# Seven products of zeros before the first scores, another order of two evictions, and twelve instead of fourteen weights prepared beside attention

## The chip, the cores and the metric

The kernel runs on one core of a Trainium2 chip. The metric is the device time of one execution in microseconds (us). PE is TensorE (matrix products; PEld is its weight load), DVE is VectorE, ACT is ScalarE, POOL is GpSimd, and SP is the engine that here issues the transfers. Each engine works through its own instructions in order and waits for others by semaphores.

## The reference, cut to what matters

Attention runs over 8 batches and 8 heads with 512 local and 32 global tokens and a head dimension of 64. A local token sees the 32 global keys and the local keys within 32 places; a global token sees all. Its result, 4608 tokens of 512 numbers, goes through two dense layers with a softplus between them.

```python
k_all = concat([k_g, k_l]); v_all = concat([v_g, v_l])
out_g = sm(scale * q_g @ k_all.T) @ v_all
s_ll = where(abs(pos[:, None] - pos[None, :]) <= 32, scale * q_l @ k_l.T, -1e9)
out_l = sm(concat([scale * q_l @ k_g.T, s_ll])) @ v_all
x = concat([out_g, out_l]).transpose(0, 2, 1, 3).reshape(4608, 512)
h = x @ w_in                                    # 512 x 2048
g = maximum(h, 0) + log1p(exp(-abs(h)))         # softplus
return g @ w_out                                # 2048 x 512
```

## The kernel before

**Stages.** Heads go in 32 pairs. The first six pairs are worked alone, before the dense layers begin; this part is called attention below. Everything behind it is the dense layers, in blocks of 512 tokens (b = 0 to 8, the last one half), with the attention of the other 26 pairs woven in between by a list of due times. In a block, 16 tiles h of 128 features are computed from x, put through the softplus, and their products with w_out are summed in four output tiles o. ORDER sets how h tiles, o products and the woven pieces follow each other.

**Products.** Results in 32 bits come from two halves: a number is split in a high part, rounded for TensorE, and a low part, the rest. Each product of x and a weight, or of g and a weight, is three: high by high, high by low, and low by high. A tile's name ends in h for its high and in l for its low part (xh, xl, gh, gl).

**The weights.** w_in and w_out come as 64-bit numbers in 32 tiles, wi0 to wi15 and wo0 to wo15. Each is prepared once: ACT takes absolute values of one word (L537, tile wbits), DVE puts the bits of a 32-bit number together in three instructions (L546, L548, L551, in the raw tile), ACT rounds them to the high part (a cast, L556), and POOL subtracts to get the low part in two instructions of 128x256 (L560). The raw words of weight k lie in the home of weight k+1 of the same kind, so weight k+1 cannot be cast before POOL has read weight k's raw words. W_PRE weights are prepared beside attention, one per step; the rest follow in block 0 of the dense layers, in the order of a list (order_w), each begun a fixed number of items ahead of its use (W_AHEAD).

**Attention's steps.** There are 15 steps, 12 local ones (pair m, half a) and three for global queries. Step k goes through stages: 0 scores on PE (two mask products, then eight products of raw queries and keys), followed by the maxima on DVE (L174, L175) and the exps with their sums on ACT (L177), 1 the reciprocals of the sums on DVE (L183, L184), 2 weighing of the exps e on POOL (L189), 3 the transpose of the weighed scores to PSUM (tile t), 4 its eviction by ACT in two parts (L223, L224: p..gh, p..gl), 5 products with the values, 6 the split of the result in xa/xh and xl (L242, L248, L249). The loop at the end of the kernel calls stages of neighbouring steps for each k; the order of these calls is the order of the work on PE and, for most of it, on ACT and DVE. The Tile scheduler places POOL's work and SP's transfers. `soft` holds the maxima and exps that belong to the scores issued in this turn of the loop, `take` is the copy of the first scores of pair 6 from PSUM (s_ps6_0, L346), and `held` is the weight whose bits are made in this step and whose cast ends it.

Of the kernel before, what the change touches and what calls it, by code (L numbers as in the profile page):

```python
# [8 lines left out]
F32 = mybir.dt.float32  # L9
F32R = mybir.dt.float32r  # L10
BF16 = mybir.dt.bfloat16
I32 = mybir.dt.int32
AF = mybir.ActivationFunctionType
ALU = mybir.AluOpType
# [25 lines left out]
SLOTS = {6: (72, 75, 78, 86, 90), 7: (81, 87, 87, 94.5, 97), 8: (93.6, 100.4, 100.4, 109, 113.5)}  # L40
ORDER = "H O H H O G O H O H H O H O G O H O H H O H O G O H O H H O H H O G O O".split()
GW = 75
W_AHEAD = 13
W_PRE = 14
LOADS = 16
START = 76
RATE = 3
# [15 lines left out]
def moe_over_global_local_attention(  # L63
# [22 lines left out]

    nc.scalar.preload_act_table_set("natural_log_exp_and_others")

    identf = pl.tile([P, P], F32, tag="e", name="identf", bufs=2)
    mask = const.tile([P, 1024], BF16, name="mask")
    ident = const.tile([P, P], BF16, name="ident")
# [34 lines left out]

    def mm(*a, **k):
        order["pe"] = after(nc.tensor.matmul(*a, **k), "pe").ins  # L130


    M = B * H // 2
# [417 lines left out]
        note("dve", nc.vector.scalar_tensor_tensor(r, lo32, 29, a, op0=ALU.logical_shift_right, op1=ALU.bitwise_or))  # L551
        return r.bitcast(F32)

    def halves_w(kind, k, r):
        (wi if kind == "wi" else wo)[k] = o = pl.tile([P, 2, 512], F32R, tag=f"{kind}{k}", name=f"{kind}{k}", bufs=1)
        i = note("act", nc.scalar.copy(o[:, 0], r))  # L556
        if not tight:
            tc.keep_in_program_order(i)
        for c in (slice(0, 256), slice(256, 512)):
            nc.gpsimd.tensor_tensor(o[:, 1, c], r[:, c], o[:, 0, c].bitcast(F32), op=ALU.subtract)  # L560

    def output_banks():
        if "o" not in banks:
# [169 lines left out]
    def stage(k, f):  # L733
        if 0 <= k < n:
            steps[k][0][f](*steps[k][1])
# [5 lines left out]
    for k in range(-2, n):  # L741
        stage(k - 3, 6)
        stage(k + 2, 0)
        soft = st.pop("soft", None)
        if soft and k:
            soft()
        stage(k + 1, 1)
        low_parts()
        stage(k + 1, 2)
        if k == 0:  # L750
            stage(k, 3)
            stage(k, 4)
            soft()
            key_masks()
        if k == n - 2:
            pcs.pop(0)[1]()
        for f, *args in fetch.get(k, ()):
            f(*args)
        if held:
            r = bits_w(*held)  # L760
        stage(k - 2, 5)
        if k == n - 1:
            stage(k - 2, 6)
            low_parts()
        if k:
            stage(k, 3)
            stage(k, 4)
        if k == n - 2:
            st.pop("take")()
        if k == n - 1:  # L770
            stage(k - 1, 5)
            stage(k - 1, 6)
            low_parts()
            pcs.pop(0)[1]()
        if held:
            halves_w(*held[:2], r)
            held = None
        if wk[1] < W_PRE:
            held = order_w[wk[1]]
            held += (abs_w(*held),)  # L780
            wk[1] += 1
# [78 lines left out]
```

## Time and profile before

| what | value |
|---|---|
| median of 3 runs | 957.56 us |
| the runs | 958.10, 957.56, 957.14 us |
| the profiled execution's own time | 957.48 us |
| its span | 955.7 us |
| granted clock, mean | 1.0 |
| PE busy | 938.4 us (98%) |
| DVE busy | 621.1 us (65%) |
| ACT busy | 506.7 us (53%) |
| POOL busy | 455.6 us (48%) |

The durations and waits come from the profiled execution. A row of the timeline has a start in us from the span's start, the busy time in us, the engine, the source line, the operation, what is written and read with its shape, a count of instructions put together (x8), and in brackets the idle time of the engine before it with what ended that. A row of the waits names who waited for whom, and gives the us in total, the number of waits and the longest. The dense layers' first product starts at 75.80 us.

### The profile page before, as it was taken

What the parts mean: (1) busy time and instruction counts of PE and PEld (TensorE: products, weight loads), DVE (VectorE), ACT (ScalarE), POOL (GpSimd) and SP (SyncE); (2) the same over time, 40 slices, a digit from 0 to 9 for tenths busy, and PEclk for the clock granted to TensorE, in tenths of its full rate; (3) what the DMA queues carried; (4) which work ended last, traced back from release to release, by engine and by line L of the source; (5) the groups of instructions that cost most, each with busy time, mean ns of one, the idle gap of its engine ahead of it and who ended that gap; (6) DMA issues with size and microseconds to landing.
All of it is one profiled execution on the core that took longest, in us unless ns stands there. A gap on an engine that the chain in (4) does not pass through costs nothing.

```text
span 955.7 us, 14401 instructions
## 1 busy us (share of the span) xinstructions
PE 938.4 (98%) x5239; PEld 757.8 (79%) x5239; DVE 621.1 (65%) x1271; ACT 506.7 (53%) x914; POOL 455.6 (48%) x634
## 2 busy tenths in 40 slices
PE   6999999999999999999999999999999999999998
PEld 4777777878888888888888888878888888888896
DVE  7985899687677667777668667767767765211211
ACT  6897776744445446444445446444445445544453
POOL 6984897654435344444435345444435334222221
PEclk9999999999999999999999999999999999999999
DMA  9745421111112110211112111211112100100000
GB/s 355 272 139 174 146 91 43 66 51 51 51 51 94 35 51 18 95 51 51 51 51 95 42 43 31 96 37 51 51 51 95 50 2 19 50 1 1 23 23 23
DMA packets 34327, 66.21 MB, mean 69 GB/s; under 512 B 7632, under 2 KB 11472, under 8 KB 34256
## 3 DMA queue, kind: packets, MB, share of 16 engines
q1 hardware_dynamic: 33440, 65.19, 20.8%
q8 instruction: 41, 0.67, 0.3%
q14 instruction: 30, 0.25, 0.1%
q10 hardware_dynamic: 816, 0.10, 0.1%
HBM read 55.84 MB, written 9.44 MB: 68 GB/s over the span
## 4 chain that ended last, share of the span: by engine, by line
PE 84%; POOL 5%; ACT 5%; DVE 4%; issue 2%; POOLq 0%; ACTq 0%; DVEq 0%
PE o L130 36%; PE h L130 35%; PE s_ps L130 5%; PE v_ps L130 5%; POOL e L189 2%; PE s L130 1%; ACT xh L509 1%; POOL gl L608 1%; POOL wi L560 1%; DVE e L603 1%; PE o0g L130 1%; PE t L130 1%; ACT e L599 1%; POOL s L416 1%; ACT gh L606 1%
## 5 line engine op out<-in xcount | busy, mean ns | idle before, releaser
L130 PE MATMUL h<-xh,wi 128*128 128x512 f32 (+1 forms) x1152 | 343.2, 381 | 0.5 <-DVE e L603 0.4
L130 PE MATMUL o<-wo,gh 128*128 128x512 f32 x1088 | 343.4, 397 | 0.0
L608 POOL TENSOR_TENSOR gl<-e,gh 128x512 fp32r<-128x512 f32 (+1 forms) x152 | 182.4, 1204 | 258.9 <-ACT gh L606 224.5
L130 PEld LDWEIGHTS h<-xh,wi 128*128 128x128 f32 x1152 | 211.4, 188 | 46.9 <-DVE e L603 1.6
L130 PEld LDWEIGHTS o<-wo,gh 128*128 128x128 f32 x1088 | 200.3, 188 | 46.3
L130 PE MATMUL h<-xl,wi 128*128 128x512 f32 (+1 forms) x576 | 219.9, 382 | 0.0
L130 PE MATMUL o<-wo,gl 128*128 128x512 f32 x544 | 213.7, 393 | 0.0
L603 DVE SCALAR_TENSOR_TENSOR e<-h,e 128x512 f32<-128x512 f32 x136 | 92.8, 682 | 172.8 <-ACT e L601 157.3
L599 ACT ACTIVATE e<-h 128x512 f32<-128x512 f32 x136 | 80.8, 594 | 213.4 <-PE h L130 213.3
L416 POOL TENSOR_TENSOR s<-s,mb 128x320 f32<-128x320 f32 (+6 forms) x136 | 138.5, 1051 | 70.9 <-DVE mb L412 70.9
L606 ACT CAST gh<-e 128x512 fp32r<-128x512 f32 x136 | 84.0, 617 | 121.9 <-DVE e L603 121.9
L130 PEld LDWEIGHTS h<-xl,wi 128*128 128x128 f32 x576 | 108.1, 188 | 21.8
L130 PEld LDWEIGHTS o<-wo,gl 128*128 128x128 f32 x544 | 102.2, 188 | 23.7 <-POOL gl L608 0.2
L601 ACT ACTIVATE e<-e,one 128x512 f32<-128x512 f32 x136 | 98.4, 724 | 4.0
L430 DVE TRANSPOSE_TENSOR_REDUCE zt<-s 128x32 f32<-128x1024 f32 x52 | 64.7, 1244 | 53.1 <-ACT s L424 53.1
L600 ACT ACTIVATE e<-e 128x512 f32<-128x512 f32 x136 | 85.9, 631 | 3.1
L424 ACT ACTIVATE s<-s 128x1024 f32<-128x1024 f32 x52 | 55.1, 1060 | 28.6 <-POOL mt L341 24.1
L365 DVE TRANSPOSE_TENSOR_REDUCE mt<-s 128x32 f32<-128x1024 f32 x52 | 64.6, 1243 | 7.7 <-ACT s L346 6.1
L390 POOL COPY mt<-mt 32x75 f32<-32x75 f32 x78 | 19.2, 246 | 96.1 <-DVE mt L365 94.0
L130 PEld LDWEIGHTS s_ps<-raw 64*128 64x128 f32 x728 | 54.9, 187 | 12.3 <-issue 8.8
L130 PE MATMUL s_ps<-raw 64*128 64x192 f32 (+3 forms) x728 | 60.6, 308 | 1.0 <-DVE e L603 0.5
L412 DVE STREAM_TRANSPOSE mb<-mt 128x512 f32<-128x512 f32 (+1 forms) x104 | 52.8, 564 | 1.2 <-ACT mt L403 0.4
(129 smaller groups left out, 863.9 us busy)
## 6 DMA issues: line engine op xcount, KB each, us to landing
raw<-in_qk SPq DMA_DIRECT2D x52, 272.0 KB, 2.8
v<-in_v SPq DMA_DIRECT2D x26, 384.0 KB, 3.1
out<-ot SPq DMA_DIRECT2D x34, 256.0 KB, 2.2
wiraw<-in_w_in SPq DMA_DIRECT2D x16, 512.0 KB, 7.2
woraw<-in_w_out SPq DMA_DIRECT2D x16, 512.0 KB, 6.6
raw<-in_qk SPq DMA_DIRECT2D x26, 224.0 KB, 3.2
v<-in_v SPq DMA_DIRECT2D x6, 512.0 KB, 7.3
raw<-in_qk SPq DMA_DIRECT2D x6, 416.0 KB, 6.2
```

What stands on the lines that cost most here:

```text
L130: order["pe"] = after(nc.tensor.matmul(*a, **k), "pe").ins
L365: order["scores"] = nc.vector.tensor_reduce(windows(st["mt", m], 4 + 16 * g, 36, 2, 16), s.rearrange("p h (b k) -> p h b k", k=32), axis=A ...
L412: nc.vector.transpose(mb[:, :, o:o + 32 * n].rearrange("p h (s k) -> p h s k", k=32), windows(e, k, 21, 2, n).unsqueeze(3).to_broadcast([P ...
L416: i = nc.gpsimd.tensor_tensor(s[:, h, o:o + w], s[:, h, o:o + w], mb[:, h, q:q + w], op=ALU.subtract)
L424: i = nc.scalar.activation(s, s, AF.Exp, scale=0.125)
L430: nc.vector.tensor_reduce(windows(st["zt", m], 4 + 16 * g, 36, 2, 16), s.rearrange("p h (b k) -> p h b k", k=32), axis=AX.X, op=ALU.add, a ...
L599: nc.scalar.activation(e, ph, AF.Abs)
L600: nc.scalar.activation(e, e, AF.Exp, scale=-1.0)
L601: nc.scalar.activation(e, e, AF.Ln, bias=one)
L603: order["e"] = nc.vector.scalar_tensor_tensor(e, ph, 0.0, e, op0=ALU.max, op1=ALU.add).ins
L606: nc.scalar.copy(gh, e)
L608: nc.gpsimd.tensor_tensor(gl[:, c], e[:, c], gh[:, c].bitcast(F32), op=ALU.subtract)
```

## The change

It has four parts.

1. A tile of zeros of 128x512 bf16 is written by DVE, and PE multiplies it seven times with itself ahead of all other products. Nothing reads the result.
2. At step k=1 the transpose and the eviction of that step are called before `soft` (the exps of step 3, e0_1_1) and before stages 1 and 2 of step 2; the second weight's cast, kept back at k=0, stands behind that eviction, and its low part on POOL behind the weighing of step 2, e0_1_0 (the order rows below have the names).
3. The copy `take` moves from step n-2 to step n-1, behind the last evictions there.
4. W_PRE goes from 14 to 12 and W_AHEAD from 13 to 11: wo4 and wo5 are no longer prepared beside attention but first in block 0.

```diff
-W_AHEAD = 13
-W_PRE = 14
+W_AHEAD = 11
+W_PRE = 12
...
+    zeros = pl.tile([P, 512], BF16, tag="mb", name="zeros", bufs=2)
+    nc.vector.memset(zeros, 0.0)
+    idle = ps_h.tile([P, 512], F32, tag="h", name="idle")
+    for _ in range(7):
+        mm(idle, lhsT=zeros[:, :P], rhs=zeros, start=True, stop=True, skip_group_check=True)
...
-    def halves_w(kind, k, r):
+    def halves_w(kind, k, r, later=None):
         (wi if kind == "wi" else wo)[k] = o = pl.tile([P, 2, 512], F32R, tag=f"{kind}{k}", name=f"{kind}{k}", bufs=1)
         i = note("act", nc.scalar.copy(o[:, 0], r))
         if not tight:
             tc.keep_in_program_order(i)
-        for c in (slice(0, 256), slice(256, 512)):
-            nc.gpsimd.tensor_tensor(o[:, 1, c], r[:, c], o[:, 0, c].bitcast(F32), op=ALU.subtract)
+        def low():
+            for c in (slice(0, 256), slice(256, 512)):
+                nc.gpsimd.tensor_tensor(o[:, 1, c], r[:, c], o[:, 0, c].bitcast(F32), op=ALU.subtract)
+
+        low() if later is None else later.append(low)
...
         soft = st.pop("soft", None)
+        behind = []
+        if k == 1:
+            stage(k, 3)
+            stage(k, 4)
+            halves_w(*kept, behind)
         if soft and k:
             soft()
         stage(k + 1, 1)
         low_parts()
         stage(k + 1, 2)
+        for low in behind:
+            low()
         if k == 0:
...
-        if k:
+        if k not in (0, 1):
             stage(k, 3)
             stage(k, 4)
-        if k == n - 2:
+        if k == n - 1:
             st.pop("take")()
-        if k == n - 1:
             stage(k - 1, 5)
             stage(k - 1, 6)
             low_parts()
             pcs.pop(0)[1]()
-        if held:
+        if held and k == 0:
+            kept = (*held[:2], r)
+        elif held:
             halves_w(*held[:2], r)
-            held = None
+        held = None
```

Line numbers of the changed kernel stand six to nine above those of before (L560 becomes L567, L608 becomes L617).

On POOL, from the weighing of the second step (e0_0_1) on, before:

```order
L189 TENSOR_SCALAR e0_0_1_173<-e0_0_1_173,sums0_1_174 128x224 x4
L560 TENSOR_TENSOR wi0_190<-wiraw0_109,wi0_190 128x256 x2
L560 TENSOR_TENSOR wi1_270<-wiraw1_117,wi1_270 128x256 x2
L189 TENSOR_SCALAR e0_1_0_203<-e0_1_0_203,sums1_0_223 128x224 x4
L560 TENSOR_TENSOR wi2_313<-wiraw2_119,wi2_313 128x256 x2
```

and of the change:

```order
L195 TENSOR_SCALAR e0_0_1_183<-e0_0_1_183,sums0_1_184 128x224 x4
L567 TENSOR_TENSOR wi0_200<-wiraw0_119,wi0_200 128x256 x2
L195 TENSOR_SCALAR e0_1_0_213<-e0_1_0_213,sums1_0_233 128x224 x4
L567 TENSOR_TENSOR wi1_303<-wiraw1_127,wi1_303 128x256 x2
L195 TENSOR_SCALAR e0_1_1_289<-e0_1_1_289,sums1_1_305 128x224 x4
L567 TENSOR_TENSOR wi2_323<-wiraw2_129,wi2_323 128x256 x2
```

The low part of wi1 has gone behind the weighing of e0_1_0, and that of wi2 behind the weighing of e0_1_1.

On ACT, at the same place (the exps of e0_1_0, weights wi1 to wi3, and the eviction of t0_0_1), before:

```order
L177 ACTIVATE e0_1_0_203,sums1_0_223<-s0_1_0_196,sums1_0_223 128x224 x4
L556 CAST wi1_270<-wiraw1_117 128x512
L537 ACTIVATE wbitswi2_274<-wiraw2_119 128x512
L177 ACTIVATE e0_1_1_283,sums1_1_284<-s0_1_1_276,sums1_1_284 128x224 x4
L223 COPY p0_0_1gh_309<-t0_0_1_300 128x512
L224 COPY p0_0_1gl_310<-t0_0_1_300 96x512
L556 CAST wi2_313<-wiraw2_119 128x512
L537 ACTIVATE wbitswi3_317<-wiraw3_127 128x512
```

and of the change:

```order
L183 ACTIVATE e0_1_0_213,sums1_0_233<-s0_1_0_206,sums1_0_233 128x224 x4
L543 ACTIVATE wbitswi2_280<-wiraw2_129 128x512
L229 COPY p0_0_1gh_299<-t0_0_1_290 128x512
L230 COPY p0_0_1gl_300<-t0_0_1_290 96x512
L562 CAST wi1_303<-wiraw1_127 128x512
L183 ACTIVATE e0_1_1_289,sums1_1_305<-s0_1_1_282,sums1_1_305 128x224 x4
L562 CAST wi2_323<-wiraw2_129 128x512
L543 ACTIVATE wbitswi3_327<-wiraw3_137 128x512
```

The eviction and the cast of wi1 now stand ahead of the exps of e0_1_1, and wi2's absolute values ahead of both.

On POOL in block 0, around the low parts of gl0_9 and gl0_10 (the softplus results of hidden tiles 9 and 10), before:

```order
L560 TENSOR_TENSOR wi14_1548<-wiraw14_1318,wi14_1548 128x256 x2
L560 TENSOR_TENSOR wo10_1624<-woraw10_1345,wo10_1624 128x256 x2
L608 TENSOR_TENSOR gl0_9_1630<-e0_9_1620,gh0_9_1629 128x256 x2
L390 COPY zt7_1561<-zt7_1561 32x75 x3
L560 TENSOR_TENSOR wo11_1675<-woraw11_1394,wo11_1675 128x256 x2
L608 TENSOR_TENSOR gl0_10_1681<-e0_10_1671,gh0_10_1680 128x256 x2
L560 TENSOR_TENSOR wi15_1685<-wiraw15_1436,wi15_1685 128x256 x2
```

and of the change:

```order
L567 TENSOR_TENSOR wi13_1612<-wiraw13_1333,wi13_1612 128x256 x2
L617 TENSOR_TENSOR gl0_9_1618<-e0_9_1608,gh0_9_1617 128x256 x2
L396 COPY zt7_1549<-zt7_1549 32x75 x3
L567 TENSOR_TENSOR wi14_1663<-wiraw14_1382,wi14_1663 128x256 x2
L617 TENSOR_TENSOR gl0_10_1669<-e0_10_1659,gh0_10_1668 128x256 x2
L567 TENSOR_TENSOR wo10_1675<-woraw10_1424,wo10_1675 128x256 x2
```

Each weight stands two places later among the weights than before; wo10 now follows gl0_10, where it preceded gl0_9.

## The prediction

> **What bounds the kernel now.** I read the page's busy shares first, then the waits of PE, then busy time by stretch.
>
> ```profile
> PE 938.4 (98%) x5239; PEld 757.8 (79%) x5239; DVE 621.1 (65%) x1271; ACT 506.7 (53%) x914; POOL 455.6 (48%) x634
> ```
>
> TensorE is busy for 938.4 of 955.7 us, so some 17 us can be saved at most, and each new PE wait costs its own length. The waits of 10 to 76 us (first row) and of 74 to 200 us (the other two, all that PE waits for there) say where these gaps are:
>
> ```profile
> PE t L130 <- POOL e L189: 4.2, 3, 2.3
> PE s_ps L130 <- DVE e L603: 0.5, 1, 0.5
> PE h L130 <- DVE e L603: 0.4, 1, 0.4
> ```
>
> Attention (to 75.8 us) is not PE's to set; from there on PE sets the time alone. In the stretches of block 0 (start:end, length, then busy us of PE, PEld, DVE, ACT, POOL):
>
> ```profile
> 75.00:85.00 10.00, 10.00 (x60) 8.48 (x59) 3.88 (x8) 6.68 (x15) 3.09 (x7) 1.00 0.81 270
> 85.00:165.00 80.00, 79.55 (x397) 62.69 (x396) 72.68 (x108) 57.75 (x101) 68.61 (x84) 1.00 0.30 96
> 165.00:180.00 15.00, 15.00 (x76) 12.13 (x75) 10.28 (x20) 9.87 (x21) 8.81 (x13) 1.00 0.12 34
> ```
>
> From 85 to 165 us DVE has 7.3 and POOL 11.4 us left of 80, while PE has no gap but the 0.4. This is where the change puts more work.
>
> **The zeros.** The first memsets stand at
>
> ```profile
> 0.83 0.15 DVE L96 MEMSET mask<- 128x112 uint32 x1 [0.83 <-PEq L851]
> 1.00 0.34 DVE L108 MEMSET mask<- 128x336 uint32 x1
> 3.92 0.91 PE L130 MATMUL s<-mask,ident 128*128 128x448 bf16 x2 [3.92 <-DVE mask L104]
> 4.76 1.86 PE L130 MATMUL s<-raw 64*128 64x224 f32 x8
> ```
>
> Clearing 128x512 bf16 (256 words a row) lies between 0.15 and 0.34 us: 0.27, so the zeros begin at about 1.25 us. Two cold mask products start 0.84 apart, 0.42 for 448 columns, so 0.48 for 512 and 3.36 for seven. They end at 4.6 and move the first scores from 3.92 by +0.7 us. Against this stands the clock:
>
> ```profile
> 7.41 1.87 PE L130 MATMUL s<-raw 64*128 64x224 f32 x8
> 9.95 0.90 PE L130 MATMUL s<-mask,ident 128*128 128x448 bf16 x2 [0.67 <-ACT e L177]
> 12.57 1.60 PE L130 MATMUL t<-identf,e 128*128 128x128 f32 x8
> 14.48 1.03 PE L130 MATMUL s<-raw 64*128 64x224 f32 x8
> ```
>
> Eight raw products take 1.87 us early and 1.03 from 14.48 on; the transposes of 12.57 hold the change, at about 13.5. The 5.4 unbroken us from 3.92 did not bring it, the 3.5 from 9.95 did. A fixed grid of equal stretches fits both: 10.0 to 13.5 full, 6.6 to 10.0 broken by the 0.67, 3.1 to 6.6 begun before 3.92. With zeros from 1.25 the stretch 3.1 to 6.6 is full, so I take full speed at 6.6; if the grid lies otherwise, between 1.25+3.5 = 4.8 and 1.25+7 = 8.3. [...]
>
> What the faster scores are worth is set by the chain behind them:
>
> ```profile
> 8.07 0.45 ACT L177 ACTIVATE e<-s,sums 128x224 f32<-128x224 f32 x1 [6.06 <-DVE sums L175]
> 9.77 0.66 ACT L537 ACTIVATE wbitswi<-wiraw 128x512 f32<-128x512 f32 x1
> 10.82 0.40 DVE L546 TENSOR_SCALAR wbitswi<-wbitswi 128x512 int32<-128x512 int32 x1
> ```
>
> The first scores, mask and raw, end 2.7 us after they start (6.6). From 4.6 with the second half at full speed they end at 6.9, 0.3 later; the exps then start at 8.37, the weight's absolute values at 10.07, and its first bits at 10.75, where before the second reduction held them to 10.82: **-0.1**. Bounds: -0.9 (full speed at 4.8), +0.7 (no change of clock). The selects of the later masks, which POOL now does behind the first mask's, and the weight loads that change places on SP go at 0: the zeros end after the first mask is there (3.92), and none of the waits of PE quoted above is for a load. If one were late, its wait would show on ACT's first pass over that weight and cost what the third weight's does below.
>
> **The second eviction.** At k=1 POOL now weighs e1_0 right behind the first weight's low part, and prepares the second low part after it.
>
> ```profile
> 18.02 0.18 DVE L184 RECIPROCAL sums<-sums 128x4 f32<-128x4 f32 x1
> 19.18 0.49 DVE L546 TENSOR_SCALAR wbitswi<-wbitswi 128x512 int32<-128x512 int32 x1 [0.98 <-ACT wbitswi L537]
> 18.65 1.61 POOL L560 TENSOR_TENSOR wi<-wiraw,wi 128x256 fp32r<-128x256 f32 x2 [0.76 <-ACT wi L556]
> 20.25 2.60 POOL L189 TENSOR_SCALAR e<-e,sums 128x224 f32<-128x224 f32 x4
> 21.78 0.68 ACT L556 CAST wi<-wiraw 128x512 fp32r<-128x512 f32 x1
> 23.08 0.76 DVE L546 TENSOR_SCALAR wbitswi<-wbitswi 128x512 int32<-128x512 int32 x1
> 21.90 1.43 PE L130 MATMUL t<-identf,e 128*128 128x128 f32 x8 [2.33 <-POOL e L189]
> ```
>
> The weighing needs the reciprocal of 18.02: 18.25 to 20.85, two us earlier, and the 2.33 of PE shrinks. Behind it the low part runs to about 22.4, and only then may ACT cast the third weight, whose home holds the second's raw values: cast to 23.1 (before 22.4), the fourth's absolute values to 23.75, and DVE's bits from 23.8 where they stood at 23.08: +0.7, with the exps behind them +0.8. ACT stands still for some 1.3 us before that cast. DVE's 0.98 goes, as the third weight's absolute values now stand ahead of the cast of the second, but DVE then meets the later stall. What it loses there lasts, because it has no slack in the stretches that follow (columns as above):
>
> ```profile
> 23.00:57.00 34.00, 30.79 (x271) 23.06 (x272) 31.48 (x60) 29.99 (x92) 29.49 (x42) 1.00 0.73 261
> 57.00:69.50 12.50, 12.50 (x112) 10.40 (x109) 11.93 (x25) 11.26 (x35) 12.03 (x18) 1.00 0.18 48
> ```
>
> DVE is busy for 31.5 of 34 us and then 11.9 of 12.5, more than PE in the first, while PE fills the second whole. So I carry the stall to the end of attention: **+0.8**. Bounds: -0.1, if DVE uses all of the saved 0.98 on work that it can draw forward and meets the later cast 0.9 late, and +1.1, if the weighing too is 0.3 later than I put it, as the low part ahead of it took 1.86 there and not the 1.6 of the others.
>
> **The last eviction and the copy.**
>
> ```profile
> 71.61 1.02 ACT L346 COPY s<-s_ps 128x1024 f32<-128x1024 f32 x1
> 72.52 0.66 ACT L242 COPY xa<-o 128x256 f32<-128x256 f32 x2
> 72.96 0.44 PE L130 MATMUL o<-p_1gh,v 128*64 128x128 f32 x4 [0.40 <-ACT xa L242]
> ```
>
> The copy of 1.02 us moves behind the xa copies, for which PE waited 0.40 at 72.96 and stood 0.17 before 71.82: **-0.55**. Bounds 0 (the gap turns to the next eviction) and -0.9 (all that the copy takes from start to start).
>
> **Two weights less beside attention.** Their bits took DVE 4.7 us in six rows, first and last:
>
> ```profile
> 62.83 0.45 DVE L546 TENSOR_SCALAR wbitswo<-wbitswo 128x512 int32<-128x512 int32 x1
> 68.48 0.82 DVE L551 SCALAR_TENSOR_TENSOR woraw<-woraw,wbitswo 128x512 int32<-128x512 int32 x1
> ```
>
> They lie where PE has no gap (12.50 of 12.50 above), so their going is worth **0**: POOL and ACT, which lose a low part of 1.5 and two passes of 0.7 us for each, are off that path as well. Without this cover, that is if DVE did set the time there, it would be up to 4.7 us gained; PE's full row excludes it. Up to the first MoE product the sum is +0.15. In block 0 the two come first and every later weight moves two places back. The places of preparation among the other work on ACT, DVE and POOL stay what they were, so I use a rule of places: a weight is ready when the weight in its place was before. Where this brings one past its use is at wo10, which falls from ahead of gl0_9 to behind gl0_10 on POOL:
>
> ```profile
> 138.96 2.08 POOL L560 TENSOR_TENSOR wi<-wiraw,wi 128x256 fp32r<-128x256 f32 x2
> 141.01 2.35 POOL L560 TENSOR_TENSOR wo<-woraw,wo 128x256 fp32r<-128x256 f32 x2
> 146.69 1.47 POOL L560 TENSOR_TENSOR wo<-woraw,wo 128x256 fp32r<-128x256 f32 x2
> 149.71 1.46 POOL L560 TENSOR_TENSOR wi<-wiraw,wi 128x256 fp32r<-128x256 f32 x2
> 149.77 0.61 PE L130 MATMUL o<-wo,gh 128*128 128x512 f32 x2
> 154.12 2.18 POOL L560 TENSOR_TENSOR wo<-woraw,wo 128x256 fp32r<-128x256 f32 x2 [0.35 <-ACT wo L556]
> 157.38 0.61 PE L130 MATMUL o<-wo,gh 128*128 128x512 f32 x2
> 140.48 1.12 DVE L548 SCALAR_TENSOR_TENSOR wbitswo<-woraw,wbitswo 128x512 int32<-128x512 int32 x1
> ```
>
> Before, wo10 (141.01) was ready at 143.4 for its products at 149.77, the second of which, at 150.0, reads the low part. Now wi14 has the place of 146.69 and wo10 that of 149.71, which ends at 151.17: PE waits 1.2 us. That is the least. The pairs took 2.08 and 2.35 beside DVE's two-input shifts (140.48, 1.12 us), and 1.47 and 1.46 elsewhere; with two more weights' shifts to do DVE is at them then. wi14 and wo10 at 2.08 and 2.35 add 1.50, so I take **+2.7**; at 2.35 both, 2.9. [...]
>
> The next, wo11, comes in the place of 154.12, ready at 156.3 for products at 157.38; those behind it are no closer. PE's stall then moves their use back by its own length, so none of them adds. The 0.41 that PE waits for a softplus near 161 is covered by the stall: **-0.4** (bound 0). DVE carries 4.7 us more through block 0, and the idle left from 165 to 180 is 4.7 of 15; what is not taken up there lands on the 0.50 that PE waits near 192, for the same engine: **+0.6** (0 to 1.2).
>
> **Sum:** -0.1 +0.8 -0.55 +2.7 -0.4 +0.6 = +3.05 on the profiled 957.48 (span 955.7 and 1.8 around it), which stands 0.08 under the median of 957.56: **960.5 us**.
>
> **Rivals.** *wo10 is not late.* From 75 to 85 us DVE has 6.1 us idle; if the two extra weights are done in it, nothing moves, the terms of block 0 are zero, and the time is 957.48+0.15 = 957.6. For it speaks that idle time and POOL's 6.9. Against it: DVE's order puts their bits behind the second softplus, which comes at 85. *The start wins (faster).* The place is DVE's row at 19.18: its 0.98 goes, and if the low part is done by 21.8, when ACT wants the cast, nothing of it comes back. With the clock's -0.9 and the copy's -0.55 attention ends 2.4 earlier, and with wo10 in time as above the time is 955.0. It decides whether POOL ends that low part before 21.8; 20.85+1.6 says not. *DVE becomes the bound (slower still).* With 72.7+4.7 = 77.4 of 80 us it has 2.6 left, and each wait of its own for ACT delays a softplus. At the upper bounds of wo10 (2.9), of the second eviction (1.1) and of block 1 (1.2), nothing gained at 161 or by the copy, the time is 957.48+5.1 = 962.6. *The zeros don't change the clock,* the case in which the change doesn't do what it says: +0.7 for -0.1 gives 961.3.
>
> **How the numbers follow.** Chances: forecast 0.55 (959.0 to 962.0 its own range), wo10 in time 0.20, the fast start 0.09, DVE the bound 0.12, no change of clock 0.04. A measurement of this kernel can tell about 0.2%, 1.9 us, from no change: under 955.6 is faster, over 959.5 slower. Faster holds the fast start, 0.09; the same holds wo10 in time and the forecast's lowest 0.06, 0.26; slower the rest, 0.65. The range of 956.6 to 962.4 leaves out most of the fast start and half of the slowest case.
>
> **What would show it.** Raw products of 1.03 us from 6.6 on; ACT idle before a cast at about 22; xa copies ahead of the s copy at 72; the first h product near 76.0 (75.8 before); and above all a PE wait of 1.2 to 2.9 us for POOL's wo row near 150. If PE shows no wait there, the forecast is wrong by its largest term; if the wait stands but the time is no longer, the start gave more than I grant.

## The result and the profile after

The changed kernel takes 964.61 us (median of 6 runs, 963.73 to 965.09), the kernel before 957.40 us on the same chip (6 runs). The ratio is 1.0073, with a 95% interval of 1.0063 to 1.0084: slower by 7.2 us. The forecast was 960.5 us, at most 962.4. The profiled execution of the change took 965.09 us, its span is 963.2.

The busy shares of the change, then all waits of PE from 74 to 205 us (PE's products stand at L130 before and at L128 in the change):

```profile
PE 940.1 (98%) x5242; PEld 758.0 (79%) x5246; DVE 624.4 (65%) x1272; ACT 506.3 (53%) x914; POOL 457.1 (47%) x634
```

```profile
PE o L128 <- POOL gl L617: 1.9, 1, 1.9
PE h L128 <- DVE e L612: 1.4, 2, 1.1
PE o L128 <- ACT gh L615: 1.1, 1, 1.1
PE s_ps L128 <- DVE e L612: 0.5, 1, 0.5
PE o L128 <- POOL wo L567: 0.2, 1, 0.2
```

PE is as busy as before but for 1.7 us, and it has four waits that it had not: for gl0_9 (1.9), for softplus results (1.1 and 0.3 beside the old 0.4 that is gone), for gh (1.1). The wait for wo10, the largest term of the forecast, is 0.2. A second loss shows in the granted clock (stretch, length, busy us of PE, PEld, DVE, ACT, POOL, clock):

```profile
85.00:145.00 60.00, 59.36 (x294) 47.02 (x296) 52.20 (x78) 42.78 (x75) 52.75 (x63) 1.00 0.32 102
145.00:165.00 20.00, 17.88 (x85) 13.66 (x84) 19.51 (x28) 13.10 (x26) 16.07 (x21) 0.91 0.19 57
165.00:180.00 15.00, 15.00 (x76) 12.13 (x75) 13.42 (x17) 11.15 (x22) 12.17 (x14) 1.00 0.23 76
180.00:205.00 25.00, 22.18 (x111) 17.06 (x110) 17.64 (x33) 13.64 (x28) 13.00 (x21) 1.00 0.22 74
```

The timeline of PE shows both losses, one behind the other:

```profile
147.62 0.50 PE L128 MATMUL o<-wo,gl 128*128 128x512 f32 x1 [1.90 <-POOL gl L617]
147.96 0.62 PE L128 MATMUL o<-wo,gh 128*128 128x512 f32 x2
...
149.81 1.05 PE L128 MATMUL o<-wo,gh 128*128 128x512 f32 x2
...
151.09 1.05 PE L128 MATMUL h<-xh,wi 128*128 128x512 f32 x2
...
152.30 0.62 PE L128 MATMUL h<-xh,wi 128*128 128x512 f32 x2
```

A pair of products takes 0.62 us, then 1.05, then 0.62 again: for some 3.4 us PE worked at half its clock (granted 0.50 from 148.79 to 152.21). From 147.96 to 152.30 it needed 4.34 us for what took 3.05 before (144.64 to 147.69), 1.29 lost.

Following the same product through both traces gives the whole sum of the change, as lateness against before: 0.61 at the first dense product (76.41 for 75.80), 0.62 more by 141 us (wait for a softplus), 2.09 at gl0_9, 1.29 by the clock, 0.51 at wo10, 0.66 back near 160 (where before PE waited 0.41), and 3.01 at two waits in the beginning of block 1 (184.56 and 191.88). That is 7.47, and from 205 us on the lateness stays at 7.5.

POOL's queue ahead of gl0_9, before and in the change:

```profile
135.77 3.19 POOL L416 TENSOR_TENSOR s<-s,mb 128x384 f32<-128x384 f32 x3
138.96 2.08 POOL L560 TENSOR_TENSOR wi<-wiraw,wi 128x256 fp32r<-128x256 f32 x2
141.01 2.35 POOL L560 TENSOR_TENSOR wo<-woraw,wo 128x256 fp32r<-128x256 f32 x2
143.33 1.63 POOL L608 TENSOR_TENSOR gl<-e,gh 128x256 fp32r<-128x256 f32 x2
```

```profile
138.82 1.94 POOL L567 TENSOR_TENSOR wi<-wiraw,wi 128x256 fp32r<-128x256 f32 x2
140.72 3.67 POOL L422 TENSOR_TENSOR s<-s,mb 128x384 f32<-128x384 f32 x3
144.39 2.04 POOL L567 TENSOR_TENSOR wi<-wiraw,wi 128x256 fp32r<-128x256 f32 x2
146.39 1.88 POOL L617 TENSOR_TENSOR gl<-e,gh 128x256 fp32r<-128x256 f32 x2
```

Before, the selects s of pair 7 ended at 138.9 and gl0_9 began at 143.33. Now wi12's low part stands ahead of these selects, wi13's behind them; the selects begin 5.0 us later than before, and gl0_9 comes 3.1 us later.

### The profile page after: what moved, and what is told of

Its sections match the earlier page's. It is cut to its first block, busy times and chain, and to the rows that moved or that the text cites. A ratio compares the mean times of both kernels' runs of the same rounds, so it can differ in the third digit from the quotient of the medians.

```text
span 963.2 us, 14406 instructions
## 1 busy us (share of the span) xinstructions
PE 940.1 (98%) x5242; PEld 758.0 (79%) x5246; DVE 624.4 (65%) x1272; ACT 506.3 (53%) x914; POOL 457.1 (47%) x634
## 4 chain that ended last, share of the span: by engine, by line
PE 82%; POOL 5%; ACT 5%; DVE 3%; issue 3%; DMA 1%; SPq 0%; POOLq 0%; ACTq 0%; DVEq 0%
PE o L128 35%; PE h L128 34%; PE s_ps L128 5%; PE v_ps L128 5%; POOL gl L617 1%; POOL s L422 1%; ACT xh L515 1%; DMA wiraw<-in_w_in 1%; PE o0g L128 1%; ACT e L608 1%; POOL wo L567 1%; PE t L128 1%; DVE e L612 1%; POOL e L195 1%; PE s L128 1%
## 5 line engine op out<-in xcount | busy, mean ns | idle before, releaser
L128 PE MATMUL o<-wo,gh 128*128 128x512 f32 x1088 | 344.6, 398 | 1.3 <-ACT gh L615 1.1
L128 PE MATMUL h<-xh,wi 128*128 128x512 f32 (+1 forms) x1152 | 343.5, 381 | 1.4 <-DVE e L612 1.4
L617 POOL TENSOR_TENSOR gl<-e,gh 128x512 fp32r<-128x512 f32 (+1 forms) x152 | 185.6, 1225 | 265.3 <-ACT gh L615 227.7
L128 PEld LDWEIGHTS h<-xh,wi 128*128 128x128 f32 x1152 | 211.8, 188 | 48.0 <-DVE e L612 2.3
L128 PEld LDWEIGHTS o<-wo,gh 128*128 128x128 f32 x1088 | 200.5, 188 | 48.4 <-ACT gh L615 1.5
L128 PE MATMUL h<-xl,wi 128*128 128x512 f32 (+1 forms) x576 | 220.0, 382 | 0.0
L128 PE MATMUL o<-wo,gl 128*128 128x512 f32 x544 | 214.4, 394 | 2.0 <-POOL gl L617 1.9
L608 ACT ACTIVATE e<-h 128x512 f32<-128x512 f32 x136 | 80.8, 594 | 211.5 <-PE h L128 210.8
L128 PEld LDWEIGHTS h<-xl,wi 128*128 128x128 f32 x576 | 108.3, 188 | 21.8
L128 PEld LDWEIGHTS o<-wo,gl 128*128 128x128 f32 x544 | 102.5, 188 | 26.4 <-POOL gl L617 2.9
L128 PEld LDWEIGHTS s_ps<-raw 64*128 64x128 f32 x728 | 54.9, 187 | 12.3 <-issue 8.8
L128 PE MATMUL s_ps<-raw 64*128 64x192 f32 (+3 forms) x728 | 60.6, 308 | 1.5 <-DVE e L612 0.5
```

The source lines that it names most:

```text
L608: nc.scalar.activation(e, ph, AF.Abs)
L617: nc.gpsimd.tensor_tensor(gl[:, c], e[:, c], gh[:, c].bitcast(F32), op=ALU.subtract)
```

## The experiments

Times are medians beside the kernel before on the same chip. As attention's end varies by itself (below), two numbers are given from each profile: where the first dense product starts (75.80 before), and how much is lost from there to the last scores of 14 products of 64x32 in block 1 (191.90 before, 116.10 behind the first dense product).

| kernel | us | before | ratio (95%) | first dense product | lost behind it |
|---|---|---|---|---|---|
| the change | 964.61 | 957.40 | 1.0063 to 1.0084 | 76.41 | 6.86 |
| weights part undone | 958.22 | 957.50 | 0.9997 to 1.0015 | 75.18 | 0.71 |
| weights part alone | 964.00 | 957.50 | 1.0053 to 1.0078 | 75.56 | 6.83 |
| order at k=1 alone | 958.45 | 957.50 | 1.0001 to 1.0019 | 76.84 | 0.66 |
| copy alone | 957.36 | 957.86 | 0.9986 to 1.0003 | 75.27 | 0.01 |
| zeros alone | 957.43 | 957.86 | 0.9986 to 1.0003 | 75.48 | 0.05 |
| change, W_AHEAD 13 | 961.11 | 957.50 | 1.0023 to 1.0048 | 76.16 | 3.77 |
| change, own scratch home | 962.13 | 957.85 | 1.0030 to 1.0061 | 75.10 | 5.35 |
| change, both of these | 962.86 | 957.86 | 1.0036 to 1.0065 | 75.83 | 5.34 |
| change, no bits for two weights | 962.61 | 957.85 | 1.0037 to 1.0065 | 76.69 | 5.13 |
| change, W_AHEAD 13, no bits | 960.87 | 957.59 | 1.0022 to 1.0049 | 76.03 | 2.85 |
| change, two low parts on ACT | 964.84 | 957.85 | 1.0060 to 1.0087 | 75.35 | 7.90 |
| change, wait filled | 963.61 | 957.59 | 1.0054 to 1.0081 | 75.49 | 6.32 |
| zeros and copy, 14 weights | 957.06 | 957.85 | 0.9983 to 1.0001 | 75.05 | 0.07 |
| the same, 15 weights | 963.94 | 957.86 | 1.0040 to 1.0069 | 76.21 | - |
| the same, 14 weights, six zeros | 956.79 | 957.59 | 0.9983 to 1.0000 | 75.06 | 0.05 |

### Which part costs

The change without its fourth part:

```diff
-W_AHEAD = 11
-W_PRE = 12
+W_AHEAD = 13
+W_PRE = 14
```

> The change with its fourth part undone: W_PRE 14 and W_AHEAD 13 as before; zeros, order of evictions and copy stay changed. Theory A (the two weights that moved into block 0 make POOL's queue late there; in the profile of the change 0.6 us are lost up to the first dense product at 76.41 and 6.9 behind it): all that lies behind 76 us is gone and 0.6 stays, 957.5 to 958.5 us, no PE wait over 0.6 us from 76 to 205 us and the granted clock 1.00 throughout. Rival B (the later or differently aligned end of attention is what makes block 0 stall): the stalls near 147, 184 and 192 us stay, over 962 us.

958.22 us. No PE wait over 0.5 us is left behind attention; one of 0.49 for gl0_9, at 144.41, is new. Theory A holds and rival B falls: the end of attention is not the cause. The kernel before with the fourth part alone (the same lines the other way):

> The kernel before with W_PRE 12 and W_AHEAD 11 and nothing else. Theory A: 957.4 + 6.9 = 964.3 us (963 to 965.5), with a PE wait for POOL's gl row of about 2 us near 147 and a stretch of lower clock behind it. Rival B: at most 959 us, as attention begins and ends as before.

964.00 us, with the wait of 1.89 for gl0_9 at 146.71 and a wait of 1.82 for wo10 at 154.13, behind which the clock drops (0.91 from 145 to 165 us). So the weights part costs 6.5 of the 7.2 us by itself. The order at step k=1 alone (the change without its zeros, with 14 and 13, and the copy at n-2):

> The kernel before with the other order at step k=1 alone (eviction before the exps, low part behind the weighing); no zeros, copy at its old place, 14 weights. By the prediction's term: +0.8 us up to the first dense product, 958.2 us, with ACT idle over 1 us ahead of the third weight's cast near 22 us. Rival: what ACT loses there DVE takes up from its saved 0.98, 957.2 to 957.5 us, as the first dense product is not later than 75.8.

+0.95 us. In its profile the first dense product is 1.04 later, and 0.66 more is lost behind it, at a wait of 0.48 for gl0_9 (146.02), which of the kernels with 14 weights only the two with this order have. That profile is of the slowest of the eleven executions (959.16 us). So the steps of the term are there, but its +0.8 agrees with the median partly by luck: some of the 0.95 is lost in block 0, where the forecast had nothing. ACT, DVE and PE of this kernel:

```profile
22.94 0.68 ACT L555 CAST wi<-wiraw 128x512 fp32r<-128x512 f32 x1 [1.73 <-POOL wi L560]
24.23 0.67 DVE L545 TENSOR_SCALAR wbitswi<-wbitswi 128x512 int32<-128x512 int32 x1 [1.71 <-ACT wbitswi L536]
26.95 1.28 PE L128 MATMUL t<-identf,e 128*128 128x128 f32 x6 [2.58 <-POOL wi L560]
```

ACT stands still for 1.73 us ahead of the third weight's cast, DVE's bits come at 24.23 for 23.08, and PE's old wait of 2.33 has only gone one step further, to 2.58 at 26.95. The copy alone, and the zeros alone (the five lines of the change that make them, put into the kernel before):

```diff
-        if k == n - 2:
+        if k == n - 1:
             st.pop("take")()
```

> The kernel before with the copy of pair 6's first scores moved behind the last evictions and nothing else. By the prediction's term: PE's wait of 0.40 for xa near 73 is gone, -0.55, 957.0 us. Rival: the wait goes to another eviction or the clock's early steps hide it, 957.4 to 957.8 us.

> The kernel before with the seven products of zeros and nothing else. Two theories on what the faster scores are worth. The prediction's: -0.1, as the chain of exps, absolute values and bits holds the same end, 957.4 us. From the profile of the change, where the first bits of a weight came at 10.15 for 10.82: -0.5 to -0.7, 956.9 us, where the load of the second weight doesn't hold ACT (it waited 0.7 for it in the profile of the change and not in that of the same kernel with 14 weights).

-0.50 and -0.43 us. Each interval just includes no change; that the first dense product comes 0.53 and 0.32 earlier agrees with both. The wait of 0.40 for xa is gone with the copy and still there with the zeros. Together, with 14 weights and without the other order at k=1:

> The kernel before with the zeros and the later copy of the first scores of pair 6, without the other order at k=1 and with 14 weights. By the terms as measured so far: the copy -0.5 (PE's wait of 0.40 for xa is gone in the profile of the change), the zeros -0.3 to -0.7 (first exps at 7.74 for 8.07, first bits at 10.15 for 10.82) unless the load of the second weight takes that up: 956.3 to 957.2 us, which would be the fastest of all. Rival: ACT's first pass over the second weight waits for its load, and the other order of attention's end costs elsewhere: 957.3 to 957.8.

957.06 for 957.85 us. The single effects (-0.50, -0.43, +0.95, +6.5) add to 6.5, and the whole change has 7.2.

### Why two weights cost six microseconds

The number of weights and the lag behind which each is begun were changed together. Lag undone, number kept:

```diff
-W_AHEAD = 11
+W_AHEAD = 13
 W_PRE = 12
```

> The whole change, but W_AHEAD 13 instead of 11, so that the two weights that are no longer prepared beside attention are both begun at the very start of block 0 and each later weight is begun at the item at which it was begun before. Theory A, as a question of load (4.7 us of DVE and 2.9 of POOL more in a stretch where DVE has 7 and POOL 11 of 80 us left): the stall at gl0_9 stays, 963 to 965 us. Rival C (a question of the lag: every weight is begun two places later than before, and that alone makes it late): the time falls to 958 to 960 us and wo10 is ready before its products.

961.11 us: between the two. 3.8 us are lost in place of 6.9. The wait for wo10, the half clock and both waits in block 1 are gone; that for gl0_9 is 0.64; new are waits for softplus results, 1.12 and 0.68 us between 109 and 117 and 0.54 at 144. What the lag does at the end of block 0 is seen on DVE, in the change and with W_AHEAD 13:

```profile
168.86 0.68 DVE L612 SCALAR_TENSOR_TENSOR e<-h,e 128x512 f32<-128x512 f32 x1
169.46 0.42 DVE L552 TENSOR_SCALAR wbitswo<-wbitswo 128x512 int32<-128x512 int32 x1
...
174.37 1.06 DVE L557 SCALAR_TENSOR_TENSOR woraw<-woraw,wbitswo 128x512 int32<-128x512 int32 x1
175.35 0.68 DVE L612 SCALAR_TENSOR_TENSOR e<-h,e 128x512 f32<-128x512 f32 x1
```

```profile
169.47 0.68 DVE L612 SCALAR_TENSOR_TENSOR e<-h,e 128x512 f32<-128x512 f32 x1
172.84 0.69 DVE L612 SCALAR_TENSOR_TENSOR e<-h,e 128x512 f32<-128x512 f32 x1 [2.69 <-ACT e L610]
```

With the lag of 11 the last two weights' bits, six instructions, stand between the softplus of h tiles 13 and 14, which are then 6.5 us apart and not 3.4. DVE has little to spare behind that (two gaps, 0.65 and 0.40 us, up to 185.9), and block 1 begins with its splits and softplus late: the 3.01 us at 184.56 and 191.88. With 13 weights ahead these bits are done before tile 13.

The end goes with DVE's lateness there, and with PE's earlier waits only as far as they make DVE late. Counted from the first dense product, DVE's softplus of tile 15 is late by 6.86 us in the change, 6.84 in the weights part alone, and 6.33, 7.91, 5.33 and 5.14 in the four kernels below that keep the lag of 11 (wait filled, two low parts on ACT, own scratch home, no bits); lost in the end are 6.86, 6.83, 6.32, 7.90, 5.35 and 5.13. From tile 13 to tile 15 this lateness grows by 3.96 to 3.99 us in all six, and by 0.01 with W_AHEAD 13. PE, by the same count, was 4.50 us late at about 164 us in the change and 6.04 in the weights part alone, and both end 6.8 to 6.9 late.

The second suspect was a home. In block 0 the scratch of wo4 and wo5 (the tiles wbits, where absolute values and bits are worked out) lies in the two homes of the transposed masks mb; with 14 weights beside attention the first to do this in block 0 are wo6 and wo7.

```diff
-            a = pl.tile([P, 512], I32, tag="mb", name=f"wbits{kind}{k}", bufs=2)
+            a = pl.tile([P, 512], I32, tag="mb" if tight or k not in (4, 5) else "wb", name=f"wbits{kind}{k}", bufs=2 if tight or k not in (4, 5) else 1)
```

> The whole change, but the scratch tiles of wo4 and wo5 in block 0 get a home of their own (one more 128x512 tile) instead of one of the two homes that the transposed masks of the woven pairs use (tag mb). Nothing is left out. Theory H (homes: in the profile of the change POOL's s<-s,mb of pair 6 begins at 90.52, before it began at 84.83, because the mask's transposes on DVE had to wait for the scratch tiles of two more weights, and POOL never catches up): the selects come back to about 86 us, the wait for gl0_9 (1.9) and the stretch of lower clock behind it (1.3) go, 960 to 962 us. Theory L (load: whatever the order, DVE has 4.7 and POOL 2.9 us more to do before 150 us): 963.5 to 965 us.

962.13 us, inside neither theory's end but nearer H: 5.35 lost for 6.86, and the first dense product happened to be 1.3 us earlier. (The select that the text puts at 84.83 before is the second; the first began at 82.62.) The mask's transpose on DVE and POOL's first selects, before, in the change and here:

```profile
81.73 1.10 DVE L412 STREAM_TRANSPOSE mb<-mt 128x512 f32<-128x512 f32 x2
82.62 0.87 POOL L416 TENSOR_TENSOR s<-s,mb 128x320 f32<-128x320 f32 x1 [3.49 <-DVE mb L412]
```

```profile
89.74 1.09 DVE L418 STREAM_TRANSPOSE mb<-mt 128x512 f32<-128x512 f32 x2
90.52 3.60 POOL L422 TENSOR_TENSOR s<-s,mb 128x320 f32<-128x320 f32 x3 [0.98 <-DVE mb L418]
```

```profile
81.04 2.02 DVE L418 STREAM_TRANSPOSE mb<-mt 128x512 f32<-128x512 f32 x4
81.93 0.87 POOL L422 TENSOR_TENSOR s<-s,mb 128x320 f32<-128x320 f32 x1 [3.49 <-DVE mb L418]
```

The home is what put these 8 us later, as DVE transposed the mask only after wo4's bits. With it cured the wait for gl0_9 is 0.95 in place of 1.9, so the home explains about half of it; no half clock follows (1.00 from 145 to 165 us), and wo10 is waited for after all, at 152.18, for 1.86 us. The two waits in block 1 (1.05 and 1.12) stay. Both cures in one kernel, the two edits above together:

> The whole change with both cures: a scratch home of their own for wo4 and wo5 and W_AHEAD 13. Singly they gave 962.1 and 961.1 for 964.6 us. If the homes and the lag are two causes that add, 958.2 to 959.2 us, what the change with 14 weights takes (958.2) plus at most 1. If the load (4.7 us of DVE) is a third cause: 960 to 961 us with PE waits for DVE's softplus between 105 and 145 us as with W_AHEAD 13 alone (1.1, 0.7, 0.5).

962.86 us: they don't add; with W_AHEAD 13 the home of its own even costs (5.34 lost for 3.77). PE waits for gl at 107 (1.08), and for softplus at 111, 117 and 145 (1.32, 0.68, 0.54). So home and lag are not two causes with prices of their own. That each only decides on which engine's queue two more weights are in front is my reading; no run shows it by itself.

Whether DVE's or POOL's load is behind it, by taking work away:

```diff
+        if not tight and kind == "wo" and k in (4, 5):
+            return hi32.bitcast(F32)
         i = nc.vector.tensor_scalar(a, a, 3, None, op0=ALU.logical_shift_left)
```

> The whole change, but DVE's three instructions for wo4 and wo5 are left out in block 0 (the raw words go to the cast as they are, so these two weights are wrong): 4.7 us of DVE less, the same work on ACT and POOL. If DVE's load is what is short: 958 to 960 us, no PE wait over 0.7 us between 76 and 205. If POOL's is: over 962.5, and the wait for gl0_9 stays over 1.5 us.

```diff
         def low():
+            if not tight and kind == "wo" and k in (4, 5):
+                nc.scalar.copy(o[:, 1], r)
+                return
```

> The whole change, but POOL's two instructions for the low parts of wo4 and wo5 in block 0 are replaced by one copy of ACT (the low part is then wrong): 2.9 us and more of POOL less, the same work on DVE, 0.7 us more on ACT for each. If POOL's queue is what is short: the wait for gl0_9 and the lower clock behind it go, 960 to 961.5 us. If DVE's load is: 963.5 to 965 us.

962.61 us without DVE's bits, 964.84 without POOL's low parts. So taking these low parts off POOL gains nothing; that its load plays no part is not quite shown, as ACT now has the copies and PE waits 0.46 us for a softplus at 113.94 where the change has no wait. Without the bits the wait for gl0_9 falls to 0.7, but wo10 (1.8) and block 1 (1.1 and 1.1) stay, nearly as with a home of their own. The mask's transpose comes at 86.93 here (89.74 in the change, 81.04 with the home) and POOL's first select at 89.15, only 1.4 us earlier than in the change: the place of the selects alone doesn't set the wait for gl0_9, and what makes up the rest of it stays open. With lag and bits both taken away:

> The whole change with W_AHEAD 13 and without DVE's three instructions for wo4 and wo5 (these two weights are then wrong). Without the bits alone: 962.6, with W_AHEAD 13 alone: 961.1. If lag (W_AHEAD) and DVE's load of 4.7 us are the two causes, both are gone here: 958 to 959 us as with 14 weights (958.2), no PE wait for DVE over 0.6 us. If the load isn't a cause of its own, the waits for DVE's softplus of W_AHEAD 13 (1.1, 0.7, 0.5) stay: 960.5 to 961.5 us.

960.87 us, with waits for DVE of 0.91 at 135.67 and 0.73 at 143.26: with W_AHEAD 13, DVE's 4.7 us account for 0.9 of the 3.8 us lost and not for the rest. From 127 to 143 us DVE does the same instructions in the same order as before, only 3.1 us later (a softplus at 134.94 for 131.81), while PE was 0.2 late; the softplus of the first tile was 0.3 late, the third 1.4, the seventh 3.1. What pushed these back with the bits gone was not taken apart.

### The half clock

```diff
                 for i, (gv, u) in enumerate(((gh, 0), (gh, 1), (gl, 0))):
                     mm(po[t], lhsT=gv[:, tsl], rhs=wo[ff][:, u], ...)
+                    if (b, f, t, i) == (0, 9, 0, 1):
+                        for _ in range(8):
+                            mm(po[t], lhsT=gh[:, tsl], rhs=wo[ff][:, 1], start=False, stop=False)
```

> The whole change, and in block 0 the second product of the first output tile with wo9 is repeated eight times ahead of the product with gl0_9 for which PE waits 1.9 us (the result is then wrong by these repeats), about 1.8 us of products at full clock in place of idle time. If the lower clock behind that wait comes from PE standing still: granted clock 1.00 from 145 to 165 us and 963.0 to 963.6 us for 964.6. If it has nothing to do with the wait: 964.4 to 965 us and the clock still under 0.95 there.

963.61 us, -1.0 with an interval that overlaps the change's. In its profile the clock is 1.00 where it was 0.91:

```profile
144.24 2.43 PE L128 MATMUL o<-wo,gh 128*128 128x512 f32 x10
146.77 0.50 PE L128 MATMUL o<-wo,gl 128*128 128x512 f32 x1
...
154.18 0.50 PE L128 MATMUL o<-wo,gh 128*128 128x512 f32 x1 [1.83 <-POOL wo L567]
```

The half clock is gone. But wo10 now makes PE wait 1.83 us: in the change the half clock had hidden this wait. Behind wo10 PE is as late as in the change (4.60 us for 4.50, counted from the first dense product); the 0.54 us less that this profile loses come in block 1, where DVE is less late. So by these two profiles the half clock's 1.29 us added nothing to the price in the end.

### Away from the change

Zeros and copy as above, with one weight more beside attention:

```diff
-W_AHEAD = 13
-W_PRE = 14
+W_AHEAD = 14
+W_PRE = 15
```

> Away from the change: zeros and the later copy, and 15 instead of 14 weights prepared beside attention (W_AHEAD 14). If two weights in block 0 cost because block 0 is short of time on DVE, one weight less there can give back at most the 0.9 us that PE still waits there (0.4 near 160 and 0.5 near 191): 956.0 to 957.1 us beside 957.1 for zeros and copy with 14. If attention has no room left for a fifteenth: 957.5 us or more, with a later first dense product.

963.94 us (960.24 to 964.80). The profile is of the fastest of the six executions, so it doesn't hold what the slower ones lose besides. In it PE waits 1.85 for xa at 73.37, and in block 0 for softplus results 1.21 and 1.19: the rival's side. One weight more beside attention, with its lag of 14, is as bad as two fewer. With 14 and one product of zeros less:

```diff
-    for _ in range(7):
+    for _ in range(6):
         mm(idle, lhsT=zeros[:, :P], rhs=zeros, start=True, stop=True, skip_group_check=True)
```

> Zeros and later copy with 14 weights as in the fastest kernel so far (957.06), but six products of zeros instead of seven. The seventh ends at 4.27, the first mask is there at 3.9: six let the scores begin 0.4 us earlier if the clock changes as early as with seven: 956.6 to 957.0 us. Rival: one product less leaves the first full stretch short more often, and the clock changes one stretch (3.4 us) later in some executions: 957.0 to 957.6 us.

956.79 for 957.59 us (0.9983 to 1.0000), the fastest kernel of all, and with seven zeros 957.06 for 957.85: both are 0.8 us faster than the kernel before, with intervals that just reach no change. Six and seven can't be told apart.

## Why the prediction was wrong, point by point

- **What bounds the kernel**: held in the main. Attention is not PE's to set, and nothing that happened behind 205 us mattered. That each new PE wait costs its own length held for a wait alone, not for several: what PE lost early, wo10 or block 1 did not take again (4.50 or 6.04 us late at 164 us, the same end).
- **The zeros** (-0.1, bounds -0.9 and +0.7): the zeros begin at 1.31 and end at about 4.3, the score products are at full clock from about 5.5 (forecast 6.6), and the first bits come at 10.15 for 10.82. Alone they give -0.43, with an interval that reaches no change. The mechanism and sign held; the size was off since the clock came 1.1 us earlier than taken, so that the first exps start 0.33 us earlier than before (7.74 for 8.07) and not 0.3 later, and the second reduction no longer holds DVE.
- **The second eviction** (+0.8): +0.95, by the steps given up to the first dense product; the agreement in size is partly luck, as 0.66 of the 1.70 us that its profile loses lie in block 0.
- **The copy** (-0.55): -0.50, by the steps given; the interval just includes no change.
- **Attention's end** (+0.15): +0.61 in the profile of the change. The same instructions gave 75.10 to 76.69 in other profiles; see the last section.
- **Two weights less beside attention** (0 there): held, as the weights part alone has its first dense product at 75.56, within the spread.
- **wo10** (+2.7, range 1.2 to 2.9): one of two steps that failed, in its rule of places: "The places of preparation among the other work on ACT, DVE and POOL stay what they were". They didn't. wo4's scratch took a home of the masks, the selects of pair 6 came 8 us later, and the first thing that PE missed was gl0_9, a place ahead of wo10: 2.09 us, and 1.29 at half clock. A home of their own for the scratch takes away about half of the wait for gl0_9; the rest of it stays open. Behind these 4.6 us of lateness wo10 was nearly in time (0.51). Where no half clock comes ahead of wo10, the forecast's wait is there and in its range: 1.86 us with a home of their own, 1.83 with the wait filled, 1.82 in the weights part alone and without the bits. The 1.50 in it for longer pairs on POOL was my estimate from four rows of one profile, and no run varies DVE's shifts alone; in the change wo10's pair took 2.41 us (2.35 in the estimate) with two-input shifts of DVE at 153.70 and 154.59, and wi14's 1.45 (2.08 in the estimate) with none beside it. The order of DVE's work at the start of block 0 had the new place of the scratch before any run:

```
L612 SCALAR_TENSOR_TENSOR e0_1_1070<-h0_1_1055,e0_1_1070 128x512
L552 TENSOR_SCALAR wbitswo4_1062<-wbitswo4_1062 128x512
L554 SCALAR_TENSOR_TENSOR wbitswo4_1062<-woraw4_576,wbitswo4_1062 128x512
L557 SCALAR_TENSOR_TENSOR woraw4_576<-woraw4_576,wbitswo4_1062 128x512
L552 TENSOR_SCALAR wbitswo5_1083<-wbitswo5_1083 128x512
L418 STREAM_TRANSPOSE mb6_0_1121<-mt6_940 128x2x256
```

  wo4's bits stand ahead of the transpose mb6_0, which came right behind the first softplus before. The trace of the change has it so: bits from 86.64 on, the transpose at 89.74. I read the order for one of the rivals and not for its effect on POOL.
- **The softplus near 161** (-0.4): held; the wait of 0.41 is gone, and 0.66 us of lateness with it.
- **Block 1** (+0.6, to 1.2): 3.01, the other step that failed and the larger miss. Right in the place and in the engine, DVE; mis-sized, because I counted idle time and not order. DVE's idle time from 165 to 180 us, 4.7, was mostly filled (13.42 busy for 10.28), but with the bits of two weights ahead of a softplus: DVE's lateness against before is 3.50 us at the softplus of tile 13, 6.64 at tile 14 and 7.48 at tile 15. PE was 4.46 late by then and had to wait for the difference.
- **The clock in block 0**: not in the forecast at all. I used the clock for the start alone.
- **The rivals**: "wo10 is not late" came true in its words and not in its time. "DVE becomes the bound" (962.6) was nearest, with 5.1 us for the 7.2 measured: it held the waits on DVE, not the queue of POOL nor the clock. "The start wins" and "the zeros don't change the clock" fell: attention ended 0.61 us later, and the clock came early. That the load is what costs fell for the most part: with DVE's 4.7 us taken away 2.85 to 5.13 us of loss remain.

## What to carry to other kernels

Work that is moved takes its scratch homes with it: look up which other tile shares the home at the new place, and follow the one that then waits, before any sum over load. On engines that work in order, as DVE did here with wo4's bits (86.64 us) ahead of the transpose listed behind them (89.74), count what stands ahead of the late instruction, not the idle time of the stretch. A pair of tuned numbers (how many are prepared early, how far ahead the rest is begun) is a pair: 12 and 11, 12 and 13, 15 and 14 were all 3 to 7 us slower than 14 and 13.

## What the runs showed of the hardware

**A wait of under 2 us can cost PE its full clock, and where it falls decides.** Behind waits of 1.8 to 1.9 us in block 0 the clock fell to half for some 3.4 us three times (behind gl0_9 in the change and with two low parts on ACT, behind wo10 with the weights part alone) and stayed full four times (gl0_9 with the weights part alone, wo10 with a home of its own, without bits, and with the wait filled). Where products filled the wait for gl0_9, it stayed full behind it (1.00 from 145 to 165 us, 0.91 in the change). I had counted only the wait. What sets these nearly equal waits apart is seen in the traces. In each of them the granted clock changes only at points that lie whole multiples of 3.41 us apart (in the change at 5.43, 148.79, 152.21 and 961.16 us), which cut the execution into equal stretches. In the weights part alone one wait of 1.89 us lies across two stretches (144.82 to 146.71, 1.57 of it in the first row), the next of 1.82 within one (third row). Start:end, length, then busy us of PE, PEld, DVE, ACT, POOL, and the granted clock:

```profile
145.14:148.55 3.41, 1.84 (x8) 1.53 (x9) 3.37 (x4) 1.85 (x4) 3.26 (x6) 1.00 0.00 0
148.55:151.96 3.41, 3.41 (x17) 2.71 (x15) 3.36 (x8) 3.38 (x7) 3.33 (x6) 1.00 0.74 235
151.97:155.38 3.41, 1.58 (x7) 1.05 (x6) 3.41 (x6) 1.66 (x6) 2.10 (x2) 1.00 0.00 0
155.38:158.79 3.41, 3.41 (x13) 2.30 (x13) 3.34 (x4) 3.13 (x6) 3.04 (x5) 0.50 0.01 2
```

| wait in block 0 | us | most of it in one stretch | clock behind it |
|---|---|---|---|
| gl0_9, the change | 1.90 | 1.90 | half |
| gl0_9, two low parts on ACT | 1.86 | 1.86 | half |
| wo10, weights part alone | 1.82 | 1.82 | half |
| gl0_9, weights part alone | 1.89 | 1.57 | full |
| wo10, own scratch home | 1.86 | 1.45 | full |
| wo10, wait filled | 1.83 | 1.42 | full |
| wo10, no bits | 1.82 | 0.91 | full |

All 17 traces agree, from the first change of the clock to 900 us: the clock was half in the stretch behind each in which PE stood still for 1.69 us or more, 17 of them, and in no other (at most 1.67). Of the 17, three are those of the table, 13 lie in attention, in as many profiles, behind a wait of 1.9 to 2.6 us that ends between 20 and 27 us, and one behind a wait at 8.3 us (the change with both cures). PE's transposes count as work here: in the profile of before, PE stood still for 1.44 us of the stretch from 20.46 to 23.87, another 1.27 us held transposes alone, and the clock stayed full.

**The clock's first change differs from one execution to the next.** Without zeros the raw products reached full speed at about 13.5 us in the profile of before and by 10 us in that of the weights part alone, with the same PE instructions up to there:

```profile
10.78 1.86 PE L130 MATMUL s<-raw 64*128 64x224 f32 x8
```

```profile
10.41 1.03 PE L130 MATMUL s<-raw 64*128 64x224 f32 x8
```

The other two without zeros changed at 13.56 (order alone) and 7.31 us (copy alone). The spacing of the grid that I read from one profile held (3.5 us read, 3.41 measured), but where it lies was one draw of several. With the zeros the change came between 4.0 and 6.6 us in all 13 profiles (in one, the change with both cures, the clock fell back to half between 10.0 and 13.4 us). Up to this first change the traces record no clock, and the clock column of a stretch shows 1.00 there, though eight raw products take 1.86 us there and 1.03 behind it.

**What is late next at the start is a load.** ACT reached the second weight before its raw words in nine of the sixteen profiles taken beside that of the kernel before, by 0.2 to 0.8 us, as in the change:

```profile
13.68 0.67 ACT L543 ACTIVATE wbitswi<-wiraw 128x512 f32<-128x512 f32 x1 [0.69 <-DMA wiraw<-in_w_in]
```

Nine profiles have zeros, order and copy as in the change. Attention ended at 76.03 to 76.69 in the four where ACT waited for this load, and at 75.10 to 75.83 in the other five. This is the spread of 1.6 us that makes effects of half a microsecond hard to tell here; that the load causes the whole of it is not shown. In the profile of before ACT waits for no load there, and the forecast, which read the loads from it alone, set them at 0.
